# Feature 128 by one matmul and a gather through DRAM; the other second-stage matmuls four to a unit, odd half first

## Chip, cores and metric

One NeuronCore of a Trainium2 chip runs the whole program. The metric is the time of one execution on the device in microseconds; the time of a kernel is the median of several runs. Beside the runs there is one profiled execution, with every instruction and every DMA packet. TensorE is PE in the profile, VectorE DVE, ScalarE ACT, GpSimd POOL, and SyncE, which here only issues DMAs, SP.

## What is computed

```python
X = np.fft.fft(x, axis=1)          # x: 8 batches, 3008 residues, 256 features
X = np.fft.fft(X, axis=2).real
t = X.reshape(8 * 3008, 256)
g = t @ w_gate                     # 256 x 1536
out = (gelu(g) * (t @ w_val)) @ w_out
```

The input x and the output are float32. The matmuls run in bf16.

## The kernel before

**The transform.** A batch has T = 3008 rows of C = 256 features. x is first folded along the features (`fold_x`): each feature f and its mirror 256 - f give a sum ("even", features 0 to 128) and a difference ("odd", 1 to 127). The odd half's column 0 has no odd feature of its own, so it carries feature 128, which belongs to the even kind. The 3008 rows are taken as 64 x 47. The first stage of the sequence transform (`a_step`, twelve per batch, bank ps_d or ps_o) multiplies by G and leaves S in SBUF. S goes to DRAM (`z_write`, four DMAs each after steps 5 and 11) and comes back transposed as Ap (`z_read`, two DMAs of 16 of the 32 groups each): 96 partitions x 32 groups x 256 features.

**The second stage** (`b_steps(b, eo, q)`) makes Y, 128 features x (even and odd) x 1505 columns, from Ap. A quarter q is eight groups. For every group and half, one matmul with 128 columns of Ap as weights and 47 columns of a table (TP for even, TQ for odd, T0P and T0Q for group 0, which has an additional matmul of one column) writes 47 columns of a PSUM bank. For the odd half, eight more matmuls (nine in quarter 0) with one weight column each ("m1") overwrite partition 0 with feature 128, by the even table. `evac` copies the bank into Y with columns reordered: ACT copies for all batches but the first. The bank is ps_d, of which there is one.

**The feed-forward part.** The 1505 columns of a batch are three chunks (512, 512, 481), and w_gate and w_val, multiplied beforehand by the feature transform, are cut in 12 columns of 128. A unit u is a (batch, chunk, fc); 36 units make a batch, 288 the program. The matmuls of a unit stand in `layer1` (line 465): five of up to 512 columns in a unit of kind 1, six in one of kind 0. Kind 1 saves one matmul and instead has DVE use NQ, which is feature 128's row of Y spread over 128 partitions. ACT applies Gelu (lines 486 and 497), DVE and POOL multiply (501, 510, 524). The result h goes through w_out in `l2_steps` (line 549): eight matmuls of 256 columns at the end of each unit, 24 for an output tile. ACT copies the tile into osb (line 560, four buffers), and SP stores it by four or five DMAs (line 529).

**What sets the order.** The loop at line 622 writes all units one after the other, and `pin` keeps the order of PE, ACT, DVE and POOL as written from there on. SP's DMAs are placed by the scheduler, early where their data permit. While the units of batch b run, x of batch b + 2 is loaded and folded (POOL), the first stage of batch b + 1 runs in units 0 to 11, and z is read back in units 12 and 13. The second stage of batch b + 1 is given out as "fills" in units 18 to 33, four units to a quarter: four even matmuls, four even matmuls and the eviction, eight odd, eight m1 and the eviction. Two fills at a time stand between the L465 matmuls. After unit 33, `spread_n` writes partition 0 of the odd half of Y to DRAM and reads it back spread over NQ. The second stage of batch 0 runs ahead of the loop.

A DMA on SP waits on SP until its data are there, and what is behind it in SP's queue waits with it. SP uses eight completion semaphores in turn, so a DMA also waits for the one eight before it.

Of the kernel before, what the change touches and what calls it, by code (L numbers as in the profile page):

```python
# [9 lines left out]
FP32 = mybir.dt.float32  # L10
BF16 = mybir.dt.bfloat16
AF = mybir.ActivationFunctionType
# [6 lines left out]
def _sub(base: bass.AP, free_pattern, free_offset, part_start=0, part_num=None):  # L19
    p_step, p_count = base.ap[0]  # L20
    if part_num is None:
        part_num = p_count - part_start
    pat = [[p_step, part_num]] + [list(x) for x in free_pattern]
    off = base.offset + part_start * p_step + free_offset
    return ap_replace(base, ap=pat, offset=off)
# [3 lines left out]
def kernel(  # L29
# [20 lines left out]
    nc = tc.nc  # L50

    B, T, C = x.shape
    F = moe_w_gate.shape[1]
    N1, N2 = 64, 47
    NJ = 48
    HJ = 24
    NG = 32
    NCH = C // 128
    NFC = F // 128
    NCOL = T // 2 + 1  # L60
    YW = NCOL + 1
    CH = [(0, 512), (512, 512), (1024, NCOL - 1024)]
    MID = 24

    const_pool = ctx.enter_context(tc.tile_pool(name="const", bufs=1))
    work = ctx.enter_context(tc.tile_pool(name="work", bufs=1))
    psum = ctx.enter_context(tc.tile_pool(name="psum", bufs=1, space=bass.MemoryType.PSUM))
    dram = ctx.enter_context(tc.tile_pool(name="dram", bufs=1, space=bass.MemoryType.DRAM))

    G = const_pool.tile([128, HJ, 128], BF16)  # L70
    TP = const_pool.tile([2 * NJ, 2 * N2], BF16)
    TQ = const_pool.tile([2 * NJ, 2 * N2], BF16)
    T0P = const_pool.tile([2 * NJ, NJ], BF16)
    T0Q = const_pool.tile([2 * NJ, NJ], BF16)
    CW = const_pool.tile([128, NCH, 2, 128], BF16)
    WE = const_pool.tile([128, 2, F], BF16)
    WOP = const_pool.tile([128, 2, F], BF16)
# [16 lines left out]
    rowq = const_pool.tile([128, 64], FP32)  # L94
    rowt = const_pool.tile([128, 4 * N2 + 2 * NJ], FP32)
    quat = const_pool.tile([128, 4 * N2 + 2 * NJ], FP32)
    rowc = const_pool.tile([128, C], FP32)
    quac = const_pool.tile([128, C], FP32)

    def xin_tile():  # L100
        return work.tile([128, 8, C], FP32, tag="xin", bufs=3, name="xin")
# [34 lines left out]
    def ps_d():  # L136
        return psum.tile([128, 512], FP32, tag="d", bufs=1, name="ps_d")
# [7 lines left out]
    def pin(ins):  # L145
        return tc.keep_in_program_order(ins) if held[0] else ins
# [71 lines left out]
    for k in range(2):  # L218
        iota(_sub(rowt, [[1, 2 * N2]], k * 2 * N2), [[1, 2 * N2]], 0, 0)
        iota(_sub(rowt, [[1, MID]], 4 * N2 + k * NJ), [[1, MID]], 0, 0)  # L220
        iota(_sub(rowt, [[1, MID - 1]], 4 * N2 + k * NJ + MID), [[1, MID - 1]], 1, 0)

# [103 lines left out]
        nc.vector.tensor_copy(WNb[:, :], ps[:, :NFC])  # L326
        nc.vector.tensor_copy(WN[:, :], WNb[:, :])

    def spread_n(b):
        Y = Ys[b]  # L330
        row = dram.tile([1, YW], BF16, tag="nrow", bufs=2, name="nrow")
        nc.sync.dma_start(out=row[:, :NCOL], in_=_sub(Y, [[1, NCOL]], YW, 0, 1))
        nc.sync.dma_start(
            out=NQ[b % 2][:, :NCOL],
            in_=ap_replace(row[:, :], ap=[[0, 128], [1, NCOL]], offset=row[:, :].offset))


    st = [dict() for _ in range(B)]
    Ys = [None] * B
# [42 lines left out]
    def b_steps(b, eo, q):  # L382

        box = {}

        def mm(gi, m1):
            def run():
                if "ps" not in box:
                    box["ps"] = ps_o() if b == 0 and eo else ps_d()
                ps = box["ps"]  # L390
                Ap = st[b]["Ap"]
                g = 8 * q + gi
                w = _sub(Ap, [[1, 1 if m1 else 128]], g * C + eo * 128)
                even = m1 or eo == 0
                o = gi * N2
                r = slice(0, 1) if m1 else slice(0, 128)
                if g == 0:
                    t = T0P if even else T0Q
                    pin(nc.tensor.matmul(ps[r, 0:N2], w, t[:, 0:N2], start=True, stop=True))  # L399
                    pin(nc.tensor.matmul(ps[r, 8 * N2 : 8 * N2 + 1], w, t[:, N2 : N2 + 1],  # L400
                                         start=True, stop=True))
                else:
                    s = (36 * g) % N2
                    t = TP if even else TQ
                    pin(nc.tensor.matmul(  # L405
                        ps[r, o : o + N2], w, t[:, s : s + N2], start=True, stop=True))
            return run

        def evac():
            ps = box["ps"]  # L410
            if Ys[b] is None:
                Ys[b] = Y_tile()
            Y = Ys[b]
            g0 = 8 * q

            def copy(o, i):
                if b:
                    pin(nc.scalar.activation(o, i, AF.Copy))
                else:
                    nc.vector.tensor_copy(o, i)  # L420

            copy(
                _sub(Y, [[32, MID], [1, 8]], eo * YW + g0),
                _sub(ps, [[1, MID], [N2, 8]], 0))
            n2 = N2 - MID
            f = 1 if q == 0 else 0
            copy(
                _sub(Y, [[32, n2], [1, 8 - f]], eo * YW + 32 * MID + g0 + f - 1),
                _sub(ps, [[1, n2], [N2, 8 - f]], MID + f * N2))
            if q == 0:  # L430
                copy(
                    _sub(Y, [[32, n2]], eo * YW + 32 * MID + 31), ps[:, MID:N2])
                copy(
                    _sub(Y, [[1, 1]], eo * YW + NCOL - 1), ps[:, 8 * N2 : 8 * N2 + 1])

        steps = [mm(gi, False) for gi in range(8)]
        if eo == 1:
            steps += [mm(gi, True) for gi in range(8)]
        return steps, evac

# [166 lines left out]
            load_x(1, i)  # L607
    for i in range(3):
        fold_x(1, i, nc.gpsimd)
    for q in range(4):  # L610
        for eo in range(2):
            steps, evac = b_steps(0, eo, q)
            for s in steps:
                s()
            evac()
    spread_n(0)

    NU = len(units)
    PER = NU // B
    l2q = []  # L620
    held[0] = True
    for u in range(NU + 2):
        b, i = divmod(u, PER)
        fills = []
        after = None
        if u < NU:
            open_unit(u)
            if i % 12 == 0 and b + 2 < B:
                load_x(b + 2, i // 12)
            if b + 1 < B:  # L630
                if 18 <= i < 34:
                    k = i - 18
                    q, r = divmod(k, 4)
                    if r == 0:
                        st[b + 1]["cur"] = b_steps(b + 1, 0, q)
                    elif r == 1:
                        after = st[b + 1]["cur"][1]
                        fills = st[b + 1]["cur"][0][4:]
                    elif r == 2:
                        st[b + 1]["cur"] = b_steps(b + 1, 1, q)  # L640
                    if r == 0:
                        fills = st[b + 1]["cur"][0][:4]
                    elif r == 2:
                        fills = st[b + 1]["cur"][0][:8]
                    elif r == 3:
                        fills = st[b + 1]["cur"][0][8:]
                        after = st[b + 1]["cur"][1]
        fills = list(fills)

        def fill(most=2):  # L650
            for _ in range(most):
                if fills:
                    fills.pop(0)()

        def second(n):
            for _ in range(n):
                if l2q:
                    l2q.pop(0)()

        if u < NU:  # L660
            val_even(u)
            fill()
        if 0 < u <= NU:
            gate_minus(u - 1)
            fill()
        if u < NU:
            gate_plus(u, fill)
            if banks[u]["kd"] == 0:
                plus(banks[u])
        if 0 < u <= NU:  # L670
            val_odd(u - 1)
        while fills:
            fill()
        if after:
            after()
        if u > 1:
            minus(u - 2)
        if u < NU:
            if i % 12 >= 4 and b + 2 < B:
                fold_x(b + 2, i // 12, nc.gpsimd, i % 12 - 4, 1)  # L680
            if b + 1 < B:
                if i < 12:
                    for k in [i] if b else [2 * i - 12, 2 * i - 11]:
                        if k >= 0:
                            a_step(b + 1, k)
                            if k % 6 == 5:
                                z_write(b + 1, 2 * (k - 5), 12)
                elif i in (12, 13):
                    z_read(b + 1, 16 * (i - 12), 16)
                if i == 33:  # L690
                    spread_n(b + 1)
        if 0 < u <= NU and u % 12 == 0:
            pb, pi = divmod(u // 12 - 1, 3)
            l2q += l2_steps(pb, pi)
        second(8 if u <= NU else len(l2q))
# [30 lines left out]
```

## Time and profile before

| | |
|---|---|
| median of 3 runs | 703.01 us (702.57 to 703.59) |
| profiled execution | 703.29 us, span 701.3 us |
| granted PE clock | 0.990 |
| DMA | 82.44 MB in 64794 packets, mean 118 GB/s |
| second-stage matmuls, 128 weight columns | 496 + 16 on L405 and L399, 16 on L400 (by weight loads) |
| m1 matmuls, one weight column | 248 + 8 on L405 and L399, 8 on L400 |

The span runs from the first to the last instruction of the profiled execution. A row of a group gives line, engine, operation, tiles, shapes and count, then busy time and mean duration, then the idle time before the instructions and what ended it. A row of a timeline gives start, duration, engine, line, operation, tiles and count; in brackets the idle time before it and what ended it. Matmuls are pipelined: their durations overlap, and the pace of PE is read from their starts. "96*1" is a weight load of 96 rows and one column.

### The profile page before, as it was taken

How to read it: one execution, taken by the hardware profiler on the slowest of the kernel's cores; microseconds unless marked ns; L12 is line 12 of the kernel's file. 1: busy time of each engine (PE TensorE's matmuls, PEld its weight loads, DVE VectorE, ACT ScalarE, POOL GpSimd, SP SyncE). 2: the span in 40 equal slices, each digit the busy share in tenths (PEclk: the TensorE clock that was granted, in tenths of full speed). 3: DMA queues.
4: the chain of work that ended last, by engine and by line, in shares of the span. 5: the costliest groups of instructions: out<-in, count | busy, mean ns of one | idle time of the engine just before them, and what ended most of it. 6: DMA issues, size and time to landing. Idle time of an engine off the chain costs nothing.

```text
span 701.3 us, 14428 instructions
## 1 busy us (share of the span) xinstructions
PE 659.1 (94%) x4848; PEld 421.5 (60%) x4848; DVE 540.3 (77%) x896; ACT 450.5 (64%) x937; POOL 407.6 (58%) x681
## 2 busy tenths in 40 slices
PE   1479789999999999999999999999999999999997
PEld 0144456666666666666666666666666666666666
DVE  7848757689776987788776987779776887689891
ACT  2447556676667766686667766676667766666662
POOL 1309665667673885847774876747764353415451
PEclk9989989999999999999999999999999999999999
DMA  8898844547434564356434475165312371211112
GB/s 182 267 234 175 200 124 106 145 115 182 118 76 116 124 171 118 71 135 160 119 95 118 102 190 125 46 156 126 90 41 61 81 180 39 59 46 44 45 47 72
DMA packets 64794, 82.44 MB, mean 118 GB/s; under 512 B 8392, under 2 KB 58568, under 8 KB 60624
## 3 DMA queue, kind: packets, MB, share of 16 engines
q1 hardware_dynamic: 62624, 77.59, 44.8%
q10 hardware_dynamic: 544, 3.15, 1.3%
q0 software_dynamic: 1552, 0.79, 0.9%
q8 instruction: 38, 0.62, 0.4%
q14 instruction: 36, 0.29, 0.1%
HBM read 45.03 MB, written 37.25 MB: 117 GB/s over the span
## 4 chain that ended last, share of the span: by engine, by line
PE 87%; DMA 7%; DVE 3%; SPq 1%; POOL 1%; issue 1%; ACT 0%; ACTq 0%; DVEq 0%; POOLq 0%
PE ps_o L549 35%; PE ps_g L465 26%; PE ps_v L465 19%; PE ps_d L405 4%; DMA xin<-in_x_dram 4%; DMA Ap<-z 2%; PE ps_d L353 2%; SPq L370 1%; DMA z<-S 1%; DVE xf L183 0%; DVE S L359 0%; PE ps_d L399 0%; DVE xf L182 0%; POOL xf L182 0%; POOL xf L183 0%
## 5 line engine op out<-in xcount | busy, mean ns | idle before, releaser
L524 POOL TENSOR_TENSOR h<-gl,dv 128x512 bf16<-128x512 bf16 (+1 forms) x216 | 246.9, 1143 | 232.8 <-DVE dv L515 194.0
L549 PE MATMUL ps_o<-Wo_sb,h 128*128 128x256 bf16 (+2 forms) x2304 | 297.3, 273 | 0.0
L501 DVE TENSOR_TENSOR h<-gl,ps_v 128x512 bf16<-128x512 bf16 (+1 forms) x288 | 192.4, 677 | 122.1 <-ACT gl L497 77.1
L486 ACT ACTIVATE gl<-ps_g 128x512 bf16<-128x512 f32 (+1 forms) x288 | 169.4, 588 | 165.9 <-PE ps_g L465 139.9
L549 PEld LDWEIGHTS <-h 128*128 128x128 bf16 (+2 forms) x2304 | 227.9, 100 | 61.1 <-issue 1.2
L497 ACT ACTIVATE gl<-ps_g 128x512 bf16<-128x512 f32 (+1 forms) x288 | 168.8, 586 | 17.8 <-PE ps_g L465 17.8
L476 DVE SCALAR_TENSOR_TENSOR ev<-nq,WN,ps_v 128x512 f32<-128x512 bf16 (+1 forms) x216 | 157.8, 731 | 3.8 <-PE ps_v L465 2.5
L515 DVE SCALAR_TENSOR_TENSOR dv<-ev,ps_v 128x512 f32<-128x512 f32 (+1 forms) x216 | 144.3, 668 | 0.0
L465 PE MATMUL ps_v<-Y,WE 128*128 128x512 bf16 (+1 forms) x288 | 108.5, 377 | 0.8 <-DVE h L510 0.4
L465 PE MATMUL ps_v<-Y,WOP 128*128 128x512 bf16 (+1 forms) x288 | 108.6, 377 | 0.0
L465 PE MATMUL ps_g<-Y,WOP 128*128 128x512 bf16 (+1 forms) x288 | 108.5, 377 | 0.0
L465 PE MATMUL ps_g<-Y,WOM 128*128 128x512 bf16 (+1 forms) x288 | 108.4, 376 | 0.1
L465 PE MATMUL ps_g<-Y,WE 128*128 128x512 bf16 (+1 forms) x288 | 108.4, 376 | 0.0
L182 POOL TENSOR_TENSOR xf<-xin 128x127 bf16<-128x127 f32 (+3 forms) x148 | 72.6, 491 | 23.0 <-DMA xin<-in_x_dram 22.2
L465 PEld LDWEIGHTS <-WOP 128*128 128x128 bf16 x576 | 55.9, 97 | 45.9 <-issue 2.6
L405 PEld LDWEIGHTS <-Ap 96*128 96x128 bf16 (+1 forms) x744 | 49.2, 93 | 55.5 <-issue 30.6
L183 POOL TENSOR_TENSOR xf<-xin 128x127 bf16<-128x127 f32 (+3 forms) x148 | 72.8, 492 | 0.0
L465 PEld LDWEIGHTS <-WE 128*128 128x128 bf16 x576 | 56.2, 97 | 27.0 <-issue 1.7
L560 ACT ACTIVATE osb<-ps_o 128x512 f32<-128x512 f32 x80 | 47.8, 597 | 30.0 <-PE ps_o L549 26.5
L510 DVE TENSOR_TENSOR h<-gl,ps_v 128x512 bf16<-128x512 bf16 (+1 forms) x72 | 48.5, 673 | 6.4 <-PE ps_v L465 6.2
L405 PE MATMUL ps_d<-TP,Ap 96*128 96x47 bf16 (+1 forms) x465 | 48.6, 186 | 1.7 <-DMA Ap<-z 1.6
L358 ACT ACTIVATE S<-ps_d 128x512 bf16<-128x512 f32 x74 | 44.7, 604 | 1.2 <-PE ps_d L353 1.2
(91 smaller groups left out, 328.5 us busy)
## 6 DMA issues: line engine op xcount, KB each, us to landing
out_dram<-osb SPq DMA_DIRECT2D x360, 64.0 KB
xin<-in_x_dram SPq DMA_DIRECT2D x40, 512.0 KB
z<-S SPq DMA_DIRECT2D x64, 192.0 KB
Ap<-z SPq DMA_DIRECT2D x16, 768.0 KB
xin<-in_x_dram SPq DMA_DIRECT2D x8, 448.0 KB
nq<-nrow SPq DMA_DIRECT2D x8, 376.2 KB
wst<-in_moe_w_gate_dram ACTq DMA_DIRECT2D x1, 1536.0 KB
wst<-in_moe_w_val_dram ACTq DMA_DIRECT2D x1, 1536.0 KB
```

Of the source, the lines that this page charges most:

```text
L182: pin(eng.tensor_tensor(ea, lo, hi, op=ALU.add))
L183: pin(eng.tensor_tensor(od, lo, hi, op=ALU.subtract))
L405: pin(nc.tensor.matmul(ps[r, o : o + N2], w, t[:, s : s + N2], start=True, stop=True))
L465: pin(nc.tensor.matmul(ps[:, :n], W[:, i, r["fs"]], r["Y"][:, eo, r["c0"] : r["c0"] + n], start=start, stop=True, skip_group_check=not start))
L476: pin(nc.vector.scalar_tensor_tensor(r["ev"][:, :nm], r["nq"][:, r["c0"] : r["c0"] + nm], WN[:, fc : fc + 1], r["pv"][:, :nm], op0=ALU.mul ...
L486: pin(nc.scalar.activation(r["glm"][:, : r["nm"]], r["pg"][:, : r["nm"]], AF.Gelu))
L497: pin(nc.scalar.activation(r["glp"][:, :n], r["pg"][:, :n], AF.Gelu))
L501: pin(nc.vector.tensor_tensor(r["h"][:, r["fc"], :n], r["glp"][:, :n], r["pv"][:, :n], op=ALU.mult))
L510: pin(nc.vector.tensor_tensor(hm, r["glm"][:, :nm], pv[:, :nm], op=ALU.mult))
L515: pin(nc.vector.scalar_tensor_tensor(dv[:, :nm], r["ev"][:, :nm], 2.0, pv[:, :nm], op0=ALU.mult, op1=ALU.subtract))
L524: pin(nc.gpsimd.tensor_tensor(hm, r["glm"][:, :nm], r["dv"][:, :nm], op=ALU.mult))
L549: pin(nc.tensor.matmul(ps[:M, s * C : (s + 1) * C], h[:, fc, sign * 512 + sub * 128 : sign * 512 + sub * 128 + M], Wo_sb[:, fc, :], start= ...
```

## The change

The m1 matmuls stay for batch 0 only. For the others, `n_step` computes feature 128 of all 32 groups by one matmul: its weights are feature 128 of the 32 groups (32 columns, C apart), its moving operand TW, 436 columns. TW holds TP repeated with period 47 over 388 columns, and T0P behind it; since group g needs the table from offset 36 g mod 47, it finds its 47 columns at an offset that falls by 11 from group to group. `gen_tw` builds TW on POOL. ACT copies the 32 x 436 result to Pn, SP writes it to DRAM (D), and five DMAs gather the right 1505 elements of D, two bytes each, into a row in DRAM. `spread_n` reads this row into NQ, and `n_row` writes it into partition 0 of the odd half of Y, after the odd half has been evicted.

The fills are given out by a written plan. For batches 2 to 7: odd quarters in units 18-19, 20-21, 23-24, 25-26, four matmuls to a unit, `n_step` at the end of unit 22, and even quarters in 27 to 34, four to a unit. For batch 1, during batch 0: odd quarters of eight matmuls in units 22, 23, 25 and 26, `n_step` in 24, the even ones as above. The constants rowc and quac move into buffers of the work pool, under the tag of gl, to make room.

```diff
+    SH = 11 * (NG - 1)
+    PW = SH + N2 + NJ
...
+    def gen_tw():
+        lead = SH % N2
+        nc.gpsimd.tensor_copy(TW[:, :lead], TP[:, N2 - lead : N2])
+        nc.gpsimd.tensor_copy(
+            _sub(TW, [[N2, SH // N2 + 1], [1, N2]], lead),
+            _sub(TP, [[0, SH // N2 + 1], [1, N2]], 0))
+        nc.gpsimd.tensor_copy(TW[:, SH + N2 :], T0P[:, :])
...
-    def spread_n(b):
-        Y = Ys[b]
-        row = dram.tile([1, YW], BF16, tag="nrow", bufs=2, name="nrow")
-        nc.sync.dma_start(out=row[:, :NCOL], in_=_sub(Y, [[1, NCOL]], YW, 0, 1))
+    def spread_n(b, row):
         nc.sync.dma_start(
             out=NQ[b % 2][:, :NCOL],
             in_=ap_replace(row[:, :], ap=[[0, 128], [1, NCOL]], offset=row[:, :].offset))
...
+    def n_step(b):
+        ps = ps_d()
+        pin(nc.tensor.matmul(
+            ps[:NG, :PW], _sub(st[b]["Ap"], [[C, NG]], 128), TW[:, :], start=True, stop=True))
+        pin(nc.scalar.activation(Pn[:, :], ps[:NG, :PW], AF.Copy))
+        D = dram.tile([NG, PW], BF16, tag="D", bufs=2, name="D")
+        nc.sync.dma_start(out=D[:, :], in_=Pn[:, :])
+        row = st[b]["row"] = nrow_tile()
+        d0, r0 = D[:, :].offset, row[:, :].offset
+
+        def gather(dst, src, do, so):
+            nc.sync.dma_start(
+                out=ap_replace(row[:, :], ap=dst, offset=r0 + do),
+                in_=ap_replace(D[:, :], ap=src, offset=d0 + so))
+
+        n2 = N2 - MID
+        g1 = PW - 11 + SH
+        gather([[32, MID], [1, NG - 1]], [[1, MID], [PW - 11, NG - 1]], 1, g1)
+        gather([[32, n2], [1, NG - 1]], [[1, n2], [PW - 11, NG - 1]], 32 * MID, g1 + MID)
+        gather([[32, MID], [1, 1]], [[1, MID], [1, 1]], 0, SH + N2)
+        gather([[32, n2], [1, 1]], [[1, n2], [1, 1]], 32 * MID + 31, SH + N2 + MID)
+        gather([[1, 1]], [[1, 1]], NCOL - 1, SH + 2 * N2)
+        spread_n(b, row)
+
+    def n_row(b):
+        row = st[b]["row"]
+        nc.sync.dma_start(out=_sub(Ys[b], [[1, NCOL]], YW, 0, 1), in_=row[:, :NCOL])
...
-        if eo == 1:
+        if eo == 1 and b == 0:
             steps += [mm(gi, True) for gi in range(8)]
...
+    evens = {27 + 2 * q + h: [(0, q, 4 * h, 4 * h + 4)] for q in range(4) for h in range(2)}
+    first = {22: [(1, 0, 0, 8)], 23: [(1, 1, 0, 8)], 24: ["n"],
+             25: [(1, 2, 0, 8)], 26: [(1, 3, 0, 8)]}
+    later = {22: ["n"]}
+    for q, i0 in enumerate((18, 20, 23, 25)):
+        for h in range(2):
+            later[i0 + h] = [(1, q, 4 * h, 4 * h + 4)]
+    plan = [first | evens, later | evens]
```

MID is 24, N2 is 47, so `n2` is 23; NG is 32. In an entry of a plan, (1, q, lo, hi) is the odd half's quarter q, matmuls lo to hi; "n" is `n_step`.

More of the change, by code (lines that the diff above doesn't have):

```diff
@@ L74 @@
     T0Q = const_pool.tile([2 * NJ, NJ], BF16)
+    TW = const_pool.tile([2 * NJ, PW], BF16)
+    Pn = const_pool.tile([NG, PW], BF16)
     CW = const_pool.tile([128, NCH, 2, 128], BF16)
@@ L96 @@
     quat = const_pool.tile([128, 4 * N2 + 2 * NJ], FP32)
-    rowc = const_pool.tile([128, C], FP32)
-    quac = const_pool.tile([128, C], FP32)
+    rowc = work.tile([128, C], FP32, tag="gl", bufs=8, name="rowc")
+    quac = work.tile([128, C], FP32, tag="gl", bufs=8, name="quac")
     def xin_tile():
@@ L327, in gen_w, with nrow_tile @@
         nc.vector.tensor_copy(WN[:, :], WNb[:, :])
-    def spread_n(b):
-        Y = Ys[b]
-        row = dram.tile([1, YW], BF16, tag="nrow", bufs=2, name="nrow")
-        nc.sync.dma_start(out=row[:, :NCOL], in_=_sub(Y, [[1, NCOL]], YW, 0, 1))
+    def gen_tw():
[5 more added lines that the diff above has]
+        nc.gpsimd.tensor_copy(TW[:, SH + N2 :], T0P[:, :])
+    def nrow_tile():
+        return dram.tile([1, YW], BF16, tag="nrow", bufs=2, name="nrow")
+    def spread_n(b, row):
         nc.sync.dma_start(
@@ L335, in spread_n, with n_first @@
             in_=ap_replace(row[:, :], ap=[[0, 128], [1, NCOL]], offset=row[:, :].offset))
+    def n_first(b):
+        row = nrow_tile()
+        nc.sync.dma_start(out=row[:, :NCOL], in_=_sub(Ys[b], [[1, NCOL]], YW, 0, 1))
+        spread_n(b, row)
[19 more added lines that the diff above has]
+        gather([[1, 1]], [[1, 1]], NCOL - 1, SH + 2 * N2)
+        spread_n(b, row)
+    def n_row(b):
+        row = st[b]["row"]
+        nc.sync.dma_start(out=_sub(Ys[b], [[1, NCOL]], YW, 0, 1), in_=row[:, :NCOL])
     st = [dict() for _ in range(B)]
@@ L609 @@
         fold_x(1, i, nc.gpsimd)
+    gen_tw()
     for q in range(4):
@@ L615 @@
             evac()
-    spread_n(0)
+    n_first(0)
     NU = len(units)
     PER = NU // B
+    evens = {27 + 2 * q + h: [(0, q, 4 * h, 4 * h + 4)] for q in range(4) for h in range(2)}
[6 more added lines that the diff above has]
+    plan = [first | evens, later | evens]
     l2q = []
@@ L624 @@
         fills = []
-        after = None
+        tail = None
         if u < NU:
@@ L630 @@
             if b + 1 < B:
[L631 to L648, printed above, removed]
+                for what in plan[min(b, 1)].get(i, ()):
+                    if what == "n":
+                        tail = lambda b=b: n_step(b + 1)
+                        continue
+                    eo, q, lo, hi = what
+                    if lo == 0:
+                        st[b + 1]["cur"] = b_steps(b + 1, eo, q)
+                    fills += st[b + 1]["cur"][0][lo:hi]
+                    if hi == 8:
+                        tail = st[b + 1]["cur"][1]
+                        if eo == 1 and q == 3:
+                            tail = lambda b=b, e=tail: (e(), n_row(b + 1))
         def fill(most=2):
@@ L673 @@
             fill()
-        if after:
-            after()
+        if tail:
+            tail()
         if u > 1:
@@ L689 @@
                     z_read(b + 1, 16 * (i - 12), 16)
-                if i == 33:
-                    spread_n(b + 1)
         if 0 < u <= NU and u % 12 == 0:
```

## The prediction

> **What bounds the kernel now.** I read the shares on the page first, then the chain of work that ended last, then TensorE's (PE's) timeline around the code that changes.
>
> ```profile
> PE 659.1 (94%) x4848; PEld 421.5 (60%) x4848; DVE 540.3 (77%) x896; ACT 450.5 (64%) x937; POOL 407.6 (58%) x681
> ...
> PE 87%; DMA 7%; DVE 3%; SPq 1%; POOL 1%; issue 1%; ACT 0%; ACTq 0%; DVEq 0%; POOLq 0%
> ```
>
> PE is busy 94% and holds 87% of the chain, so I price the change in PE time. I take a unit to run from its first `ps_v<-Y,WE` matmul to the next unit's. In batch 1 (0-based), which computes Y of batch 2:
>
> ```profile
> 187.23 0.37 PE L465 MATMUL ps_v<-Y,WE 128*128 128x481 bf16 x1
> 187.52 0.21 PE L405 MATMUL ps_d<-TP,Ap 96*1 96x47 bf16 x2
> 187.66 0.38 PE L465 MATMUL ps_g<-Y,WOM 128*128 128x480 bf16 x1
> 187.97 0.21 PE L405 MATMUL ps_d<-TP,Ap 96*1 96x47 bf16 x2
> 188.11 0.38 PE L465 MATMUL ps_g<-Y,WE 128*128 128x481 bf16 x1
> ...
> 190.10 0.37 PE L465 MATMUL ps_v<-Y,WE 128*128 128x481 bf16 x1
> 190.30 0.21 PE L405 MATMUL ps_d<-TP,Ap 96*128 96x47 bf16 x2
> 190.36 0.36 PE L465 MATMUL ps_g<-Y,WOM 128*128 128x480 bf16 x1
> ...
> 192.09 0.37 PE L465 MATMUL ps_v<-Y,WE 128*128 128x481 bf16 x1
> ...
> 208.47 0.37 PE L465 MATMUL ps_v<-Y,WE 128*128 128x481 bf16 x1
> ...
> 210.36 0.37 PE L465 MATMUL ps_v<-Y,WE 128*128 128x481 bf16 x1
> ```
>
> The unit at 208.47 has no fill and takes 1.89 us. The one at 190.10 has four 128-column fills and takes 1.99: 0.025 each. The one at 187.23 has eight one-column fills ("96*1", the m1 matmuls that the change removes) and takes 2.87: 0.98 more, 0.12 each. The durations (0.21 for a pair either way) hide this; the starts show it. A wide L465 and its pair advance PE by 0.26 us (190.10 to 190.36), a wide one and an m1 pair by 0.45 (187.66 to 188.11).
>
> PE also stands still once, in unit 18 of batch 0:
>
> ```profile
> 83.26 0.38 PE L465 MATMUL ps_v<-Y,WE 128*128 128x512 bf16 x1
> 89.66 0.22 PE L399 MATMUL ps_d<-T0P,Ap 96*128 96x47 bf16 x1 [6.02 <-DMA Ap<-z]
> ...
> 91.52 1.74 PE L549 MATMUL ps_o<-Wo_sb,h 128*128 128x256 bf16 x8
> 93.10 0.38 PE L465 MATMUL ps_v<-Y,WE 128*128 128x512 bf16 x1
> ```
>
> The first fill waits for Ap. After the wait the eight L549 take 1.74 us instead of 1.03 to 1.04: the granted clock over 83.26 to 93.10 is 0.65. The unit takes 9.84 us; the same unit of batch 1 takes 2.08.
>
> **The change part by part.**
>
> *m1 removed.* 7 batches x 33 = 231 matmuls, in four units per batch. These units take 11.77 us in batch 1; the same four in batch 7, which has no fills, 7.83. So 3.94 us a batch.
>
> *Fills spread.* Units 18 to 34 take 39.21 us in batch 1 and 32.94 in batch 7: all fills cost 6.27 us, so the wide ones and their stalls cost 6.27 - 3.94 = 2.33. Afterwards the later batches have 16 units of four fills at 0.105, plus 0.04 for the two extra N=1 matmuls of group 0: 1.72. The bank ps_d is single, so each new quarter waits for the eviction before it. Today that shows in the eight-fill units after an even quarter: 2.38, 2.27, 2.22 and 2.22 us against 1.95, 1.92, 1.89 and 1.89 unfilled, where eight (once nine) fills at 0.025 explain 0.2: stalls of 0.19, 0.14, 0.13 and 0.13. Afterwards there are seven boundaries. One lies behind the matmul for feature 128 and one starts in a six-matmul unit, where the eviction has more time: I take nothing for these. The five others cost 0.19 + 4 x 0.13 = 0.71.
>
> *One matmul for feature 128.* It streams 436 columns with 32 weight columns: 0.18 us, from the 0.20 us pace of the 481-column L465. No row shows a 32-column weight load. Below, it costs what a wide one does, 0; above, 0.25 around it, what an m1 pair adds to an L465. I take 0.2, the nearer row, since it too fills few columns: 0.38. Together 1.72 + 0.71 + 0.38 = 2.81 instead of 6.27: **3.46 us a batch, 20.8 for batches 1 to 6**.
>
> *Batch 0.* The first fill moves from unit 18 to 22. PE reaches unit 22 at 83.26 + 4 x 1.95 = 91.1; the Ap that it needs had landed by 89.66, so the wait and its slow clock go: 9.84 - 2.08 = 7.76. The fills (four units of eight, eight of four) come to about 2.7 by the same prices: 3.6 less. **11.4.** What is late next is POOL: its own wait for xin at 81.5 to 85.15 leaves it some two units behind, and dv has three buffers. By its 2.1 us a unit I find dv just free when asked for, and take 0.3 off.
>
> *What hides the rest.* The three table copies stand on POOL before the folds of batch 1, in its 18.5 us of idle until xin lands at 51.78. The copy into Pn (seven, about 0.5 us) goes to ACT, 64% busy. DVE needs about 1.75 us in a 481-column unit (steps of 0.57, 0.56 and 0.62 between its starts), below the 1.99 that a filled unit keeps; without this cover PE would be held to DVE's pace. ACT evictions stay as many.
>
> *The gather.* Each batch adds on SP: a write of D (28 KB), five gathers out of it, the spread into nq, and a row into Y, eight DMAs for two. Two gathers move 744 and 713 elements of 2 bytes, each to an address of its own. In the changed program's SP order the spread waits for the gathers, and behind it stand the last two stores of the osb tile evicted after unit 23, the row for Y, and all later stores. How many engines carry a gather? The page counts tiny packets:
>
> ```profile
> DMA packets 64794, 82.44 MB, mean 118 GB/s; under 512 B 8392, under 2 KB 58568, under 8 KB 60624
> ...
> nrow<-Y SPq DMA_DIRECT2D x8, 2.9 KB
> out_dram<-osb SPq DMA_DIRECT2D x8, 1.0 KB
> ```
>
> 547 DMAs with one completion packet on each of 16 engines would make 8752. There are 360 fewer: 24 x 15, just the 24 DMAs whose outer dimension is 31 or 1. In the packet records a 31-row store runs alone, one 1 KB packet every 42 ns from 188.37 to 190.28. So a DMA with 31 outer rows uses one engine; I expect the same of the gather with 23.
>
> Its time is G = 2.3 us to land (the longest wait of nq for nrow) + 713 x e. The trace has no 2-byte element. Below, e = 9 ns, the 4-byte packets: G = 8.7. Above, 42 ns: G = 32. I take 9 to 17, nearest in size to the 4-byte packets. Cover in batches 1 to 6: the gathers start about 4.7 us after unit 22 begins; the row is needed at unit 36, and the osb tile at the end of 35, each some 28.4 us after unit 22 begins. Less 3.3 us for issue and landing of what is behind: **G up to 20 us (e = 25 ns) is hidden.** In batch 0 the gathers stand behind stores of the tile evicted after unit 26: up to 14.5 us (e = 17 ns).
>
> Two rules of the Trainium skill speak against this step. "DMA: Bandwidth & Descriptors", section "Rules for kernel authors", says that a strided last dimension becomes one descriptor per element; no run here has one. The same page, section "Why a DMA increments its semaphore by 16 and not by 1", gives the engines as the largest number up to 16 that divides both outer sizes; the 360 missing packets agree. Its section "Bandwidth" has about 10.5 ns per small packet: an estimate of 7.5 us for 713, which would be hidden.
>
> *Sum.* 703.29 (the profiled execution: span 701.3 and 2.0 around it) - 20.8 - 11.4 + 0.3 = 671.4; the median of the runs, 703.01, lies 0.3 lower. **671 us.**
>
> **Rivals.**
>
> 1. *Slower: the narrow gather becomes the bound.* Beyond the cover, every us of G holds SP, then the stores, then osb, ACT and PE; the row for Y is late too. The 32 us of gain are gone where 6(G - 20) + (G - 14.5) = 32: G = 23.8, e = 30 ns. At 42 ns the loss is 6 x 12 + 17.5 = 90: about 760 us. For it: one engine, addresses of two bytes, reads from DRAM that the 4-byte packets do not make. Against it: packets get shorter with size (median 60 ns for 1 KB, 33 for 512 B, 9 for 4 B).
> 2. *Partly hidden.* e of 25 to 30 ns: 677 to 702 us.
> 3. *PE does not get back all.* If each of the seven boundaries costs 0.4 us, twice the largest of today, and the new matmul too, fills take 1.72 + 2.8 + 0.4 = 4.9 a batch: 671 + 6 x 2.1 = 684. Against: no stall of this kind exceeds 0.19 today.
> 4. *It does not do what it says in batch 0.* If Ap's second half, or the clock, holds PE at unit 22 or 25, up to 7.8 us stay: 679.
>
> **How the numbers follow.** Hidden gather with the stalls near today's (666 to 677): 0.68. Partly hidden, or rivals 3 and 4 (677 to 701.6): 0.12. Within 0.2% (about what a measurement can tell from no change): 0.02. Rival 1, slower: 0.18. The forecast is the likeliest case. The range leaves out rival 1 and a little below: 666 to 703; the likeliest case alone has 666 to 677.
>
> **What would show it.** Right: no "96*1" after batch 0; units 18 to 34 near 35.8 us in later batches (32.94 + 2.81); unit 18 of batch 0 at 1.95; ACT's osb evictions not waiting for stores; nq issued within some 20 us of the gathers. Wrong: SP standing at the nq spread for more than 20 us, then "ACT osb" or "PE ps_v" waiting for a DMA around unit 36; or units 19 to 33 with stalls above 0.2 us in front of the first fill.

## The result, and the profile after

The changed kernel takes **981.07 us** (median of 4 runs, 975.47 to 994.34) against 703.21 for the kernel before: a ratio of 1.3926, 95% interval 1.3827 to 1.4025. The forecast was 671.0, the range 666 to 703. One of the four runs, the longest, was disturbed and is left out of the ratio. The profiled execution takes 985.6 us, its span is 983.8.

The page of the changed kernel: busy time of the engines, DMA packets, and the chain of waits by engine:

```profile
PE 657.7 (67%) x4624; PEld 421.9 (43%) x4624; DVE 539.9 (55%) x896; ACT 452.0 (46%) x944; POOL 407.2 (41%) x684
...
DMA packets 75853, 82.63 MB, mean 84 GB/s; under 512 B 19228, under 2 KB 69628, under 8 KB 71684
...
PE 42%; SPq 32%; DMA 21%; DVE 2%; ACT 1%; issue 1%; ACTq 0%; DVEq 0%
```

PE has 224 matmuls fewer, and yet its share falls from 94% to 67%: the time is waiting. The chain, 87% PE before, is now 32% SP's queue and 21% DMA. The waits (engine, what waited for what; us in total, times, the longest) say where it meets the engines:

```profile
PE ps_v L510 <- DMA Y<-nrow: 262.3, 7, 47.4
ACT osb L605 <- DMA out_dram<-osb: 214.5, 6, 39.9
...
POOL xf L186 <- DMA xin<-in_x_dram: 158.2, 7, 54.8
```

These three are late together, so their sums are not to be added: the row for Y, the stores and the x loads all stand in SP's queue (SPq). SP's own timeline in batch 0, where the row for batch 1 is made, shows the head of that queue (start, duration, operation, count):

```profile
106.38 45.44 SPq L365 DMA_DIRECT2D nrow<-D  x5
151.87 1.73 SPq L574 DMA_DIRECT2D out_dram<-osb  x3
166.22 0.35 SPq L345 DMA_DIRECT2D nq<-nrow  x1
166.61 0.28 SPq L380 DMA_DIRECT2D Y<-nrow  x1
```

SP needs 45.44 us to issue five gathers, 39.95 of them in the third, which moves 24 elements. The spread goes out at 166.22, 59.8 us after the first gather; this time, G, is 59.4 to 63.2 us in the seven batches (forecast: 8.7 to 14.4). PE waits for the row at the start of batch 1:

```profile
170.57 0.59 PE L510 MATMUL ps_v<-Y,WOP 128*128 128x512 bf16 x1 [47.40 <-DMA Y<-nrow]
```

The packet records of a batch hold 1505 packets of two bytes; 167 to 181 of them take over 100 ns, 79 to 90 us together, and the last ends 48 to 53 us after the first gather's issue. The spread goes out 10 to 12 us after that: the semaphores of the gathers come later than the last packet record ends, and the packet records alone do not show the whole of G.

On PE the change does what it says. A unit of batch 6 with four fills:

```profile
818.55 0.38 PE L510 MATMUL ps_v<-Y,WE 128*128 128x512 bf16 x1
818.77 0.21 PE L450 MATMUL ps_d<-TQ,Ap 96*128 96x47 bf16 x2
818.83 0.38 PE L510 MATMUL ps_g<-Y,WOM 128*128 128x512 bf16 x1
819.04 0.21 PE L450 MATMUL ps_d<-TQ,Ap 96*128 96x47 bf16 x2
819.09 0.38 PE L510 MATMUL ps_g<-Y,WE 128*128 128x512 bf16 x1
...
820.61 0.38 PE L510 MATMUL ps_v<-Y,WE 128*128 128x512 bf16 x1
```

2.06 us from 818.55 to 820.61, 0.11 more than an unfilled unit. Units 18 to 34 of this batch, which nothing disturbs, take 35.92 us; the forecast was 35.75. In batch 0, unit 18 takes 1.95 us instead of 9.84, as forecast.

### The profile page after: what moved, and what is told of

It is laid out like the page before. It is cut to its first block, busy times and chain, and to the rows that moved or that the text cites. A ratio compares the mean times of both kernels' runs of the same rounds, so it can differ in the third digit from the quotient of the medians.

```text
span 983.8 us, 14054 instructions
## 1 busy us (share of the span) xinstructions
PE 657.7 (67%) x4624; PEld 421.9 (43%) x4624; DVE 539.9 (55%) x896; ACT 452.0 (46%) x944; POOL 407.2 (41%) x684
## 4 chain that ended last, share of the span: by engine, by line
PE 42%; SPq 32%; DMA 21%; DVE 2%; ACT 1%; issue 1%; ACTq 0%; DVEq 0%
SPq L365 31%; PE ps_o L594 17%; PE ps_g L510 12%; DMA nrow<-D 12%; PE ps_v L510 9%; DMA Ap<-z 4%; DMA Y<-nrow 3%; PE ps_d L398 2%; DMA D<-Pn 2%; DMA xin<-in_x_dram 1%; ACT gl L542 1%; PE ps_d L450 1%; SPq L574 0%; DMA z<-S 0%; DVE xf L187 0%
## 5 line engine op out<-in xcount | busy, mean ns | idle before, releaser
L594 PE MATMUL ps_o<-Wo_sb,h 128*128 128x256 bf16 (+2 forms) x2304 | 303.6, 277 | 0.0
L510 PE MATMUL ps_v<-Y,WOP 128*128 128x512 bf16 (+1 forms) x288 | 110.6, 384 | 262.3 <-DMA Y<-nrow 262.3
L594 PEld LDWEIGHTS <-h 128*128 128x128 bf16 (+2 forms) x2304 | 230.8, 101 | 70.7 <-issue 4.5
L605 ACT ACTIVATE osb<-ps_o 128x512 f32<-128x512 f32 x80 | 47.8, 597 | 245.5 <-DMA out_dram<-osb 214.5
L510 PEld LDWEIGHTS <-WOM 128*128 128x128 bf16 x360 | 35.8, 100 | 282.0 <-issue 268.3
L510 PE MATMUL ps_g<-Y,WOM 128*128 128x512 bf16 (+1 forms) x288 | 110.7, 384 | 4.3 <-ACT gl L542 3.0
L510 PE MATMUL ps_g<-Y,WOP 128*128 128x512 bf16 (+1 forms) x288 | 110.9, 385 | 0.0
L510 PE MATMUL ps_g<-Y,WE 128*128 128x512 bf16 (+1 forms) x288 | 110.9, 385 | 0.0
L450 PEld LDWEIGHTS <-Ap 96*128 96x128 bf16 (+1 forms) x527 | 42.1, 100 | 55.5 <-issue 23.4
```

Source lines behind the costliest of these rows:

```text
L450: pin(nc.tensor.matmul(ps[r, o : o + N2], w, t[:, s : s + N2], start=True, stop=True))
L510: pin(nc.tensor.matmul(ps[:, :n], W[:, i, r["fs"]], r["Y"][:, eo, r["c0"] : r["c0"] + n], start=start, stop=True, skip_group_check=not start))
L594: pin(nc.tensor.matmul(ps[:M, s * C : (s + 1) * C], h[:, fc, sign * 512 + sub * 128 : sign * 512 + sub * 128 + M], Wo_sb[:, fc, :], start= ...
```

## Experiments

The theory after this profile: two-byte writes side by side in DRAM are slow on the DMA engine that carries them, and SP and all that is behind it stand until they are done. Rival: the number of descriptors or the single engine is what costs. "Units 18-34" is the sum of PE's starts over these units of a later, undisturbed batch; before it was 39.21 us.

### e1: one copy in place of the gathers

```diff
-        gather([[32, MID], [1, NG - 1]], [[1, MID], [PW - 11, NG - 1]], 1, g1)
...
+        gather([[NCOL, 1], [1, NCOL]], [[NCOL, 1], [1, NCOL]], 0, 0)
```

> In place of the five gathers one contiguous copy of 3010 bytes from D to the row; every other instruction stays. Feature 128 then stands in a wrong order: the reordering is left out. Theory A (the two-byte gathers are the whole loss; fills, the matmul for feature 128 and the other DMAs cost what was forecast): 668 to 677 us, no wait of PE for Y's row, units 18 to 34 of the later batches near 35.9 us. Rival B (the longer SP queue, the switch to 32 weight columns or the new order of the halves share in the loss): over 690 us.

682.49 us (one run). G is 2.3 to 4.0 us, PE waits for no row, units 18-34 take 35.84. So some 300 us are the gathers', and the forecast of the fills is right to 0.1 us a batch. It is 11.5 us above the 671 forecast, and above the 668 to 677 expected of it, for two reasons. The loop starts at 53.1 us (48.9 before; 47.8 to 53.1 over these kernels). And unit 18 of batch 1 takes 8.89 us instead of 2.08. SP's queue in batch 1 of e1 shows why:

```profile
158.59 1.12 SPq L166 DMA_DIRECT2D xin<-in_x_dram  x2
159.81 0.99 SPq L421 DMA_DIRECT2D Ap<-z  x2
```

and then PE:

```profile
169.57 0.20 PE L440 MATMUL ps_d<-T0Q,Ap 96*128 96x47 bf16 x1 [5.05 <-DMA Ap<-z]
```

Two x loads, a megabyte, go out just ahead of Ap, which lands some 10 us after its issue; before, SP had the x loads of that batch behind Ap:

```profile
165.13 0.79 SPq L380 DMA_DIRECT2D Ap<-z  x2
165.97 7.86 SPq L529 DMA_DIRECT2D out_dram<-osb  x8
173.92 0.48 SPq L162 DMA_DIRECT2D xin<-in_x_dram  x1
```

The wait that the change takes out of batch 0 turns up in batch 1 (after: 8.71 us).

### e2: the gathers on more engines

```diff
-        gather([[32, MID], [1, NG - 1]], [[1, MID], [PW - 11, NG - 1]], 1, g1)
...
+        for m0, nm in ((0, 16), (16, 8), (24, 16), (40, 7)):
+            f = 1 if m0 < MID else 0
+            gather([[32, nm], [1, NG - 1]], [[1, nm], [PW - 11, NG - 1]], 32 * m0 + f, g1 + m0)
+            gather([[32, nm], [1, 1]], [[1, nm], [1, 1]], 32 * m0 + 31 * (1 - f), SH + N2 + m0)
```

> The same 1505 elements, but the gathers are cut into outer rows of 16, 8, 16 and 7, so that the largest share of one DMA engine falls from 713 elements to about 124 (plus a few singles). Theory A (the share of the busiest engine decides, 80 ns an element as in the changed kernel): G falls from 60 to about 12 us, under the cover of 20, and the time to 668 to 680 us. Rival B (what decides is the number of elements, whatever the engines, since they all write into the same 3 KB of DRAM: the first gather of the changed kernel, 744 elements on 12 engines, took about 13 us, 17 ns an element): G near 28 us, loss 6 x 8 + 13.5 = 62, about 735 us.

741.54 us (one run), the full computation. G falls from about 60 us to between 20.1 and 24.5 (12 or 28 were expected). Spreading helps, but it is not the cure: side by side, the elements still hold SP for 13 to 21 us. By my cover of 20 us this should have cost a few us a batch. In batches 1 to 6 PE never waits for the row, but 5 to 12 us a batch go in units 28 to 32, before the row is due, 49 us in all against e1. For batch 0, where the cover was 14.5, PE waits 10.2 us for the row. ACT and DVE, in batch 3:

```profile
374.74 0.57 ACT L542 ACTIVATE gl<-ps_g 128x481 bf16<-128x481 f32 x1
383.33 0.60 ACT L605 ACTIVATE osb<-ps_o 128x512 f32<-128x512 f32 x1 [8.01 <-remote]
```

```profile
375.34 0.66 DVE L546 TENSOR_TENSOR h<-gl,ps_v 128x481 bf16<-128x481 bf16 x1 [1.38 <-issue]
382.78 0.66 DVE L546 TENSOR_TENSOR h<-gl,ps_v 128x481 bf16<-128x481 bf16 x1 [6.78 <-remote]
```

Both stop inside the gather (362.06 to 381.7) and go on together; "remote" means that nothing on this core released them. PE's matmuls that DVE and ACT wait for had started by 377.4, but the record of their semaphores has a gap from 374.2 to 382.8, and then nine updates within 0.9 us. A fetch of instructions, 16 KB, took 3.50 us at 376.98 (median before: 1.03). What stops the engines is open; the kernel after has such stops too (batch 2: unit 29 takes 11.27 us instead of 2.20), 30 us in all against the same units of e1.

### e3: the same elements, 512 bytes apart

```diff
...
-        gather([[32, n2], [1, NG - 1]], [[1, n2], [PW - 11, NG - 1]], 32 * MID, g1 + MID)
...
+        gather([[32 * S, n2], [S, NG - 1]], [[1, n2], [PW - 11, NG - 1]], 32 * MID * S, g1 + MID)
```

with S = 256 for all five, into a buffer of its own; one element of it and a contiguous copy make the row.

> The gathers keep their shapes, but write their two-byte elements 512 bytes apart into another buffer in DRAM; the row is filled by a contiguous copy and one element of that buffer, so feature 128 is in a wrong order. Theory A1 (an element costs what it costs on one engine because it is a descriptor of its own): G stays near 60 us and the time within 950 to 1000 us. Rival A2 (neighbouring elements in the same line of memory wait for one another): the two-byte packets no longer show the waits of 400 ns, G falls below 25 us and the time below 720 us.

683.28 us (one run): the time of e1. The engines, the reads and the number of elements are those of the change; only the writes lie apart. G is 14.1 to 14.7 us, the upper end of what I forecast, no two-byte packet takes over 0.11 us, units 18-34 take 35.84. **The one narrow engine alone is not what costs; it costs when the writes lie next to each other.**

### f4: how far apart is far enough

The row by one copy as in e1, and the 713-element gather alone into a buffer nobody reads, spaced 2 bytes in batch 1, twice as far in each further batch.

```diff
+        n2, S = N2 - MID, 2 ** (b - 1)
...
+            out=ap_replace(far[:, :], ap=[[32 * S, n2], [S, NG - 1]], offset=far[:, :].offset),
```

> e1 (one copy, reordering left out) with the 713-element gather on one engine into a buffer that nobody reads, its 2-byte elements 2, 4, 8, 16, 32, 64 and 128 bytes apart in batches 1 to 7. The 512 bytes of e3 gave 17 to 19 ns an element; side by side they took about 80 on that engine. If what costs is a write into a line of 64 bytes that the write before still holds, the time falls to 20 ns at 64 bytes; if the line is 32 bytes, at 32; if it is 512, all seven stay above 40. If the cost lies in the scattered reads, it is 80 ns for all, against e3. Over all 690 to 800 us.

739.99 us (one run). From the packet records, first start to last end over 713:

| bytes apart | 2 | 4 | 8 | 16 | 32 | 64 | 128 |
|---|---|---|---|---|---|---|---|
| last packet after issue, us | 46.4 | 23.9 | 12.3 | 9.1 | 8.4 | 10.1 | 9.9 |
| ns an element | 63.1 | 31.5 | 15.3 | 10.8 | 9.7 | 9.7 | 9.7 |

The price halves with each doubling until it meets a floor of 9.7 ns at 16 to 32 bytes. Nearest to what I had written is a line of 32 bytes, but there is no step at its edge: it looks as if a write is slowed in proportion to the neighbours that share a stretch of some tens of bytes with it. The mechanism itself was not observed. The reads are the same in all seven and are cleared. The floor is near my lower end, 9 ns. It is also near the 10.5 ns a packet that the Trainium skill has ("DMA: Bandwidth & Descriptors", "Bandwidth"). The same page says under "Specifications" that below 512 bytes a DMA reads, modifies and writes; here two-byte writes 32 bytes apart already ran at the floor, so the size alone does not set the price.

These are packet records, and here too the gather's semaphore comes later. By the waits of the DMAs eight behind it, it came 63.5, 32.3 and 17.0 us after the issue at 2, 4 and 8 bytes, the first of them 17 us after the last packet. SP's waits for the gather:

```profile
SPq L577 <- DMA far<-D: 19.7, 3, 17.3
```

In batch 1 the stores behind the one slow gather were held:

```profile
106.73 0.65 SPq L380 DMA_DIRECT2D far<-D  x1
107.43 41.03 SPq L577 DMA_DIRECT2D out_dram<-osb  x2
```

The gather itself is issued in 0.65 us; it is the next DMA, here a plain store, that stands for 40 us with its issue.

### f1: the five gathers, read by nobody

```diff
+        idle = dram.tile([1, YW], BF16, tag="idle", bufs=2, name="idle")
...
-                out=ap_replace(row[:, :], ap=dst, offset=r0 + do),
+                out=ap_replace(idle[:, :], ap=dst, offset=r0 + do),
```

> The row for NQ and Y is made by one contiguous copy (reordering left out, as in e1, 682.49 us), and the five gathers of the change go, behind the row for Y, into a buffer that nobody reads. If all that the slow gather costs is that the row for Y is late, nothing waits for it now: about 683 us. If it also costs by holding SP and its engine's queue, the stores behind it are late: the gathers start some 8.5 us later than in the change, 20 us before the osb tile is needed; SP held for 45 us and some 3 us to land make 28 us a batch, 7 batches: about 880 us, with ACT's osb copy waiting for a store at the end of unit 35 and no wait of ps_v for the row, but in batch 0, where the row stands behind them. Whether ACT and DVE stop together for 4 to 10 us inside the gather, as they did with the gather on more engines, is to be read too.

978.02 us (one run). Nobody needs the gathers and the kernel is as slow as the changed one. SP from unit 27 of batch 1 on, then ACT and PE early in batch 2:

```profile
240.27 47.16 SPq L382 DMA_DIRECT2D idle<-D  x5
287.54 15.34 SPq L586 DMA_DIRECT2D out_dram<-osb  x8
```

```profile
302.50 0.60 ACT L617 ACTIVATE osb<-ps_o 128x512 f32<-128x512 f32 x1 [35.11 <-DMA out_dram<-osb]
```

```profile
304.13 0.59 PE L522 MATMUL ps_g<-Y,WOM 128*128 128x512 bf16 x1 [34.07 <-ACT gl L554]
```

There are two holds, one behind the other. The issue stands for 47 us. Then four stores go out, and the next waits from 289.3 to 301.1 for the semaphore of the second gather, eight DMAs before it. All waits of this kind:

```profile
SPq L586 <- DMA idle<-D: 79.8, 7, 12.2
```

I had expected 28 us a batch, about 880, from the first hold alone; with the second, and with the row for Y caught behind the gathers at three boundaries (130.6 us in all), it is 978.

### e4: runs of 94 bytes

```diff
+        gather([[48, NG - 1], [1, 48]], [[PW - 11, NG - 1], [1, 48]], 48, g1)
+        gather([[48, 1], [1, 48]], [[48, 1], [1, 48]], 0, SH + N2)
```

The spread then fills a buffer NR, and five ACT copies in units 31 and 33 put the order right in NQ.

> A version that computes all of it: the gather moves 32 runs of 94 or 96 bytes (31 and 1), the row is spread in that order, and five ACT copies over 128 partitions put it in order (two in unit 31, three in unit 33), then one DMA takes partition 0 into Y. Theory A: the gather is hidden, 672 to 680 us (671 to 673 as forecast, plus up to 1 us a batch of stalls from some 3 us of ACT copies). Rival (ACT copies come too late or hold Gelu): 685 to 700 us.

683.33 us (4 runs), ratio 0.9707 (0.9685 to 0.9729) to before: faster than both, though not the 672 to 680 expected. G is 2.8 to 4.8 us. Putting the order right costs ACT, in batch 1,

```profile
193.68 2.16 ACT L381 ACTIVATE nq<-nr 128x744 bf16<-128x744 bf16 x2
...
198.71 2.08 ACT L381 ACTIVATE nq<-nr 128x713 bf16<-128x713 bf16 x3
```

and PE 0.9 us a batch: units 18-34 take 36.74.

### f2: the x load behind Ap

The kernel of e1, with one further edit:

```diff
-            if i % 12 == 0 and b + 2 < B:
+            if i in (0, 14, 24) and b + 2 < B:
```

> e1 (one copy, reordering left out) with the second x load of a batch asked for two units later, so that in batch 1 both its DMAs stand behind the read of Ap instead of in front of it. If the load in front is what makes Ap late, unit 18 of batch 1 falls from 8.89 us to 2.1 and the time from 682.5 to about 675.7. If Ap is late for another reason (the z writes, the landing of Ap itself), nothing changes: 682 to 683.

681.42 us (675.96 to 682.14, 4 runs): by the time alone nothing has happened. By the profile the mechanism holds: unit 18 of batch 1 falls from 8.89 to 3.35 us. But batch 0 loses 5.5 in units 21 to 23, because POOL now waits for the later x, and PE for DVE's dv behind POOL:

```profile
93.81 0.45 POOL L186 TENSOR_TENSOR xf<-xin 128x127 bf16<-128x127 f32 x1 [10.60 <-DMA xin<-in_x_dram]
```

```profile
96.68 0.38 PE L506 MATMUL ps_v<-Y,WE 128*128 128x512 bf16 x1 [3.70 <-DVE dv L556]
```

One of the four runs, 675.96, is near the 675.7 expected; what differed in it was not profiled.

The other runs support the mechanism. Unit 18 of batch 1 takes 8.7 to 9.2 us in all six runs whose SP queue has two x loads just ahead of Ap (the changed kernel, e1, e2, e3, f1, f4), 4.2 and 4.5 in the two with one (g2, f3), and 3.1 and 3.4 in the two with none (e4, f2).

### g1 and g2: the parts by themselves

g1 is the kernel before without the m1 matmuls of batches 1 to 7:

```diff
-        if eo == 1:
+        if eo == 1 and b == 0:
             steps += [mm(gi, True) for gi in range(8)]
```

> The kernel before with the m1 matmuls of batches 1 to 7 left out, so that feature 128 of these batches is wrong; nothing else is changed, the fills stand where they stood. If m1 costs what the unit table says, 3.94 us a batch, the time is 703.6 - 7 x 3.94 = 676.0 and units 18 to 34 take 39.21 - 3.94 = 35.27 us. If part of it only fills stalls of the bank, that part stays: 680 to 690.

g2 is the changed kernel with m1 for all batches as further fills, and NQ filled from Y as before:

```diff
-        if eo == 1 and b == 0:
+        if eo == 1:
             steps += [mm(gi, True) for gi in range(8)]
...
-                    fills += st[b + 1]["cur"][0][lo:hi]
+                    steps = st[b + 1]["cur"][0]
+                    fills += steps[lo:hi] + steps[8 + lo : 8 + hi]
...
-                            tail = lambda b=b, e=tail: (e(), n_row(b + 1))
+                            tail = lambda b=b, e=tail: (e(), n_first(b + 1))
```

> The full computation with only the spreading of the change: odd half first, a quarter over two units, batch 0 from unit 22 on; the m1 matmuls stay as four more fills in each odd unit, and NQ is filled from Y as before. In batches 1 to 6 spreading alone gives nothing: 32.94 + 1.72 + 0.71 + 3.94 = 39.3 us for units 18 to 34, against 39.21. Batch 0 loses its wait of 7.8 us: about 696 us. If the read of Ap is late in batch 1 instead, as in e1 (6.8 us), the gain is given back: about 703.

g1: 677.48 us (one run), units 18-34 take 35.88. So leaving m1 out is worth 3.33 us a batch. The other 0.61 of its 3.94 turns up in the units behind the emptied ones (22, 26 and 30: 2.30, 2.18 and 2.18 us instead of 2.06, 1.99 and 1.99), where the next quarter now has to wait for the bank. g2: 694.76 us (4 runs), ratio 0.9878 (0.9848 to 0.9907); units 18-34 take 38.9 (39.21), batch 0 is 10.1 us shorter and batch 1 1.3 longer. Spreading gains almost nothing in a later batch; the start at unit 22 in batch 0 gains the rest.

### f3: the table as weights, feature 128 as one moving column

What made m1 dear, its one weight column or its size? f3 turns the matmul round: 128 columns of the table TW are the weights, one column of Ap moves. The result has the residues on partitions and the groups along a row, so that rows of 64 bytes can be written in order; 33 such matmuls a batch stand as fills beside the odd ones and use free columns of their bank.

```diff
+                    pin(nc.tensor.matmul(
+                        ps[:, 400 + j : 401 + j], TW[:, s : s + 128],
+                        _sub(Ap, [[1, 1]], gg * C + 128), start=True, stop=True))
...
+        for p0, pn, c0 in ((0, MID, 0), (MID, n2, 1)):
+            nc.sync.dma_start(
+                out=ap_replace(row[:, :], ap=[[32, pn], [1, 32]], offset=row[:, :].offset + 32 * p0),
+                in_=_sub(NP, [[1, 32]], c0, p0, pn))
```

> The full computation without a gather: feature 128 by 33 matmuls a batch with 128 columns of the table as weights and one column of Ap as the moving operand, in the free columns of the odd quarters' bank; the result has the residues on partitions, and three DMAs with runs of 64 bytes write the row in order. If the one weight column made m1 dear (0.12 us each), these cost no more than a 47-column fill with 128 weight columns (0.025): units 18 to 34 take 35.84 - 0.38 + 33 x 0.025 = 36.3 us, and the time is about 685 us or less. If any tiny matmul between wide ones costs 0.12, units 18 to 34 take 39.4 us and the time is about 704.

**674.98 us** (672.69 to 675.84, 4 runs), the full computation, ratio 0.9574 (0.9545 to 0.9603) to before: the fastest of all. A unit with four wide fills and four of these:

```profile
550.87 0.38 PE L511 MATMUL ps_v<-Y,WE 128*128 128x512 bf16 x1
551.09 0.21 PE L437 MATMUL ps_d<-TQ,Ap 96*128 96x47 bf16 x2
551.14 0.38 PE L511 MATMUL ps_g<-Y,WOM 128*128 128x512 bf16 x1
551.36 0.21 PE L437 MATMUL ps_d<-TQ,Ap 96*128 96x47 bf16 x2
551.63 0.19 PE L477 MATMUL ps_d<-Ap,TW 96*128 96x1 bf16 x2
551.68 0.38 PE L511 MATMUL ps_g<-Y,WOP 128*128 128x512 bf16 x1
551.90 0.19 PE L477 MATMUL ps_d<-Ap,TW 96*128 96x1 bf16 x2
...
553.04 0.38 PE L511 MATMUL ps_v<-Y,WE 128*128 128x512 bf16 x1
```

2.17 us, 0.11 more than the 2.06 of the unit shown above: 0.027 us for each, against 0.12 for an m1. So it was not m1's small size that cost. What is left is its one weight column, and with it the one output partition, which overwrites a result already in the bank; no run parts these two. (The Trainium skill, "TensorE: Matmul & The Clock Gate", section "Weight-path perf modes", has fast weight loads only for 128 weights. The pace agrees with it, but the records of the loads, 81 ns for one column and 99 for 128, do not show it, and no run shows that it is the reason.) Units 18-34 take 36.0, and unit 22, without the changed kernel's feature-128 matmul and its bank, 1.95 instead of 2.39 us. The 7.5 us between f3 and e1 are not PE's work, of which f3 has 0.16 us a batch more: the loop starts 3.9 us earlier, and unit 18 of batch 1 takes 4.51 us instead of 8.89.

## Why the prediction was wrong, point by point

- **What bounds the kernel; m1.** Right that PE bounds it and that m1 is dear. 3.94 us a batch was the cost in place; leaving it out gives 3.33 (g1).
- **Fills spread, one matmul for feature 128.** 2.81 us a batch forecast. Measured 2.90 (35.84 - 32.94, e1; the changed kernel has 35.92 in its undisturbed batch). The matmul for feature 128, forecast at 0.38, is 0.44 with its bank (unit 22: 2.39 against 1.95 in f3). Rival 3 is out.
- **Batch 0.** 83.46 - 72.26 = 11.2 us in e1 against 11.4. Right where I looked. That the scheduler would put x loads ahead of Ap in batch 1 stood in the changed order of SP's queue, and I did not follow the queue that far: 6.8 us given back in e1, 6.6 in the changed kernel.
- **The gather's engine.** 23 outer rows on one engine: no run speaks against it (with outer sizes of 16, 8 and 7 in e2, G is two and a half to three times shorter), but it decides only together with the price: e3 has the same shapes and is hidden.
- **The gather's price: the step that failed.** "The trace has no 2-byte element ... I take 9 to 17, nearest in size to the 4-byte packets." I bounded e by the size of packets; the upper end, 42 ns, was a 1 KB packet. By the sum that I used, (G - 2.3) / 713, e is 81 ns in the changed kernel and 86 in f4, where the gather runs without the other four (63.5 us to its semaphore): so the other gathers are not the cause. For elements far apart my range would have held (17 ns by the same sum in e3; 9.7 to 10.8 by f4's packets from 16 bytes on). What the trace of before could not show is that neighbouring destinations make a packet six times dearer (63.1 against 9.7 ns); none of the packets I priced from was such a write.
- **The cover.** "G up to 20 us is hidden" was not reached either way in the changed kernel. e3 hides up to 14.7 us in batches 1 to 6; for batch 0, where I had put the cover at 14.5, PE waits 1.8 us for the row at a G of 14.1. e2, at 20 to 24, loses more than the excess, most of it in the stops of the engines inside the gather, which I had not priced. Rival 1 had the mechanism, SP first, then osb and the row. Its slope, one us a batch for one of G, gives at G = 60: 671 + 6 x (60 - 20) + (60 - 14.5) = 957. Measured against e1, the changed kernel loses 262.3 us waiting for the row for Y (sum of 7), some 30 in the stops, and 15 in the first two units after each wait, where PE's clock is low: the granted clock is 0.50 from 170.57, where the first wait ends, to 174.74.
- **Chances.** 0.18 for rival 1 leaned on "packets get shorter with size", true of the trace of before and beside the point. The cure in the changed code was not a smaller price but contiguous runs (e4) or no reordering (f3).

Still open: what stops ACT, DVE and PE together inside a gather of neighbouring elements, that it needs such writes being shown only by its absence in e1, e3, e4 and f3; and what makes such a write slow. Not tried: e2's engines with elements far apart, and a late row for Y without SP being held.

## What to carry to other kernels

If no row shows an operation, rows that differ in what is new about it give no upper bound for its price; ask a small probe such as f4 instead of filling in from the nearest row. Do not reorder two-byte elements into neighbouring places in DRAM: let a matmul put the order on partitions (f3), or move runs and reorder on an engine (e4). A DMA's cost on a shared queue is not only when its data are due: whatever is issued behind it, whoever needs it, waits for its issue and for its semaphore's turn (f1). And a wait removed in one batch should be looked for in the next, in the order of the queue that feeds it (e1, f2).

## What the runs showed of the chip that I had not expected

- Two-byte writes to DRAM by one gather with 23 outer rows: 63.1, 31.5, 15.3 and 10.8 ns each at 2, 4, 8 and 16 bytes apart, 9.7 from 32 on (packet records of f4). At 2 bytes its semaphore came another 17 us after the last packet.
- A DMA behind a slow one stands on SP for 40 us with its issue (39.95 in the changed kernel, 41.03 for two stores in f4), though its own data are there.
- A matmul with 128 weight columns and one moving column costs PE 0.027 us between wide ones, one with one weight column and 47 moving columns 0.12 (f3, before).
